# Starting the last pass of a transformer backward kernel with the first dV chunk: blocks made earlier, delta split beside other work, copies shared by two engines

## The chip, the cores and the metric

The kernel runs on one core of a Trainium2 chip. The metric is the device time of one execution in microseconds (us). Executions of one kernel scatter here with a standard deviation of 1.3 to 3.2 us, so where a small difference matters each experiment was run in five rounds beside the kernel before on the same chip. All runs used are of the state "fast". Engines: PE is TensorE's matmul, PEld its weight load, DVE VectorE, ACT ScalarE, POOL GpSimd (it issues the stores), SP SyncE (it issues the loads).

## The reference, cut to what matters

```python
x = x + A(layernorm(x))      # grouped-query attention over a cache: 8 (batch, kv head) groups, 16384 keys, head size 128
x = x + B(layernorm(x))      # an MLP: w1 (1024 x 3584), gelu, w2
x = x + A(layernorm(x))      # the same weights and caches again
x = x + B(layernorm(x))
# returned: x and the gradients of x, K cache, V cache, wq, wo, w1, b1, w2, b2
```

The caches are 32 MB each for K and for V. They are read in several passes, and dK and dV (as large) are written in the last pass. So the kernel moves 447 MB between HBM (the chip's memory) and SBUF (a core's own).

## The kernel before, where it matters

Loads go into seven rotating tiles of 8 KB per partition (`ld`) and ten fixed ones (`res`: the chunks of K and V that stay on the chip). Small vectors lie in pools ahead of them in SBUF; the order of the pools decides the addresses.

Some terms: a chunk is 4096 keys of one group, 1 MB of K or of V. `e_all` holds the exponentials of the scores, and a block is a transposed 128x128 piece of it. dO is the gradient of the attention's output O, and delta is the sum of dO * O over the 128 elements of a head. A row of a weight matrix is 128 of its rows at once; it is turned and multiplied on PE, or done as a pair of dot products ("dots") on DVE.

```python
const = ctx.enter_context(tc.tile_pool(name="const", bufs=1))
vec = ctx.enter_context(tc.tile_pool(name="vec", bufs=1))
pers = ctx.enter_context(tc.tile_pool(name="pers", bufs=1))      # e_all
ld = ctx.enter_context(tc.tile_pool(name="ld", bufs=NLD))        # 7 tiles of 8 KB per partition
res = ctx.enter_context(tc.tile_pool(name="res", bufs=1))        # keepV0..3, keepK0..3, keepxV, keepxK
...
    def do_delta(l, dops, ahead=None):        # dO scaled, then delta = sum(dO * O), split into three bf16 parts
        ...
        doT_bf = vec.tile([128, G, 8], BF16, name=f"doT_bf{l}")
        V.tensor_copy(out=doT_bf[:], in_=dof[:])
        V.tensor_tensor(out=prod[:], in0=dof[:], in1=sv["oT"][:], op=ALU.mult)
        dlp = part_sum(prod[:].rearrange("p g r -> p (g r)"), G * 8, "dl_ps")
        ...                                   # nine DVE instructions, each on the result of the last
```

The last pass makes dV, dK and dQ of layer 0 and the weight gradients. Its head was:

```python
    for t in TP:                               # two PSUM banks
        V.memset(t[:].bitcast(F32), 0.0)
    do_delta(0, pairs(dops, HQ), wob)
    ...                                        # cols: dO of both layers side by side, by copies
    qs = [make_qm(w, order[0]) for w in "VK"]
    for c in range(NCH):
        dp = mx()[:].rearrange("p (q t) -> p q t", t=TC)
        for b in range(NB):
            scores(c, b, kept_vT(c)[:, b * 8:(b + 1) * 8, :], dp)
        ds0(c, dp)                             # needs delta
        if c == 0:
            qs[0](); make_blks(0, None)        # blocks of dV chunk 0
        elif c == 1:
            kv_pair("V", 0, 0); make_blks(1, None)
        elif c == 2:
            kv_pair("V", 0, 1); qs[1]()        # chunk 0 is now stored
        else:
            kv_pair("V", 1, 0)
    for c in range(NCH):
        for q in range(2):
            dq_quad(c, q)
        if c == 1:
            kv_pair("V", 1, 1)
    ...
    pump(NLD + 3, 4)                           # the next loads, into tiles that come free
```

`evac` helpers pick ACT or DVE by a running charge per engine; in some stretches all copies are forced onto ACT (`only["e"] = "A"`), while DVE does dot products.

## Time and profile before

| | before |
|---|---|
| three runs, us | 1165.72, 1166.01, 1171.62 |
| profiled span, us | 1165.4 |
| PE, DVE, ACT busy | 82%, 55%, 48% |
| HBM read, written | 348.14 MB, 98.58 MB |

A page of the profile divides the span into 40 slices and gives busy tenths. For one stage, the table of stretches is the better view (width, busy time and instruction count of PE, PEld, DVE, ACT and POOL, then granted clock, DMA share and GB/s). The prediction below shows and reads the lines of the hole at 745 to 765 us. One view it did not use is needed later: the packets of one stretch. Here is that line of the kernel before from 30 to 180 us, where the K and V caches stream in for the first layer's attention:

```profile
DMA packets 8604, 62.80 MB, mean 419 GB/s; under 512 B 958, under 2 KB 958, under 8 KB 958
```

The reader is to see a rate in a stretch where the DMA share is 1.01 throughout: 419 GB/s is what the 16 engines moved there.

### The profile page before, as it was taken

The page shows a single profiled execution, that of the slowest core. Times are in us where ns is not written, and L with a number is a line of the kernel's source. Part 1 is how long each engine was busy: PE and PEld are TensorE (multiplying, and loading weights), DVE is VectorE, ACT ScalarE, POOL GpSimd, SP SyncE. Part 2 cuts the span into 40 slices and gives each one's busy share as a digit, 9 for nine tenths or more (in the row PEclk, how much of TensorE's full clock was granted, in tenths as well). Part 3 has the DMA queues.
Part 4 walks back from the last instruction along what each step waited for, and adds up shares of the span by engine and source line. Part 5 has one row for each costly group of instructions (what it writes and reads, how often), then busy time and mean ns, then how long its engine had stood idle before and what let it go on. Part 6 is the DMA issues. An engine that isn't in the chain of part 4 may idle for free. (4 is left out here: it accounts for less than half of the span.)

```text
span 1165.4 us, 39945 instructions
## 1 busy us (share of the span) xinstructions
PE 955.5 (82%) x17565; PEld 733.2 (63%) x17565; DVE 639.5 (55%) x1344; ACT 562.3 (48%) x1410; POOL 63.9 (5%) x113
## 2 busy tenths in 40 slices
PE   4888895497879875889987799788998988998786
PEld 3866773487767765888776688565555554555452
DVE  1545451133545433454845355867777877787674
ACT  0544351022535430344554444467677866686673
POOL 0000000000000000000000000001111111111111
PEclk9988785587988875999998889797777877797795
DMA  9999999998999989999999999687999999999996
GB/s 370 418 419 418 419 419 397 395 360 352 418 419 414 418 306 418 388 357 408 365 414 412 338 353 350 251 325 299 374 402 422 419 419 418 420 421 418 422 419 247
DMA packets 89130, 449.30 MB, mean 386 GB/s; under 512 B 7026, under 2 KB 7026, under 8 KB 49788
## 3 DMA queue, kind: packets, MB, share of 16 engines
q1 hardware_dynamic: 72204, 348.17, 74.9%
q0 software_dynamic: 16752, 98.59, 20.6%
q8 instruction: 137, 2.24, 0.8%
q14 instruction: 37, 0.30, 0.1%
HBM read 348.14 MB, written 98.58 MB: 383 GB/s over the span
## 5 line engine op out<-in xcount | busy, mean ns | idle before, releaser
L152 ACT COPY kT<-tp 128x512 int32<-128x512 int32 x209 | 122.8, 587 | 257.5 <-PE tp L418 246.5
L155 DVE COPY kT<-tp 128x1024 bf16<-128x1024 bf16 x159 | 108.6, 691 | 112.2 <-PE tp L418 99.2
L418 PE MATMUL tp<-ident,kv_K 128*128 128x128 bf16 x1728 | 147.1, 235 | 3.5 <-DMA kv_K<-in_A_k_cache_dram 3.5
L418 PEld LDWEIGHTS <-kv_K 128*128 128x128 bf16 x1728 | 111.6, 105 | 4.1 <-DMA kv_K<-in_A_k_cache_dram 4.1
L163 DVE CAST big<-xm 128x512 bf16<-128x512 f32 (+1 forms) x138 | 89.8, 685 | 31.3 <-PE xm L1222 14.4
L160 ACT CAST big<-xm 128x512 bf16<-128x512 f32 (+1 forms) x159 | 86.7, 594 | 27.8 <-PE xm L1081 16.8
L571 PEld LDWEIGHTS <-kT 128*128 128x128 bf16 x2048 | 76.7, 98 | 28.0 <-issue 22.1
L571 PE MATMUL sc<-qT_bf,kT 128*128 128x8 bf16 x2048 | 92.1, 171 | 0.7 <-issue 0.7
L268 PE MATMUL wtp<-ident,wt 128*128 128x128 bf16 x928 | 77.1, 231 | 3.7 <-issue 2.4
L418 PE MATMUL tp<-ident,kv_V 128*128 128x128 bf16 x864 | 70.3, 227 | 10.0 <-DMA kv_V<-in_A_v_cache_dram 8.2
L304 PEld LDWEIGHTS <-wt 128*128 128x128 bf16 x1696 | 49.0, 103 | 46.0 <-issue 14.7
L535 ACT ACTIVATE e_all<-sc,negm 128x64 bf16<-128x64 f32 x256 | 77.2, 345 | 1.2 <-DVE negm L530 1.2
L163 DVE CAST keepK<-xm 128x512 bf16<-128x512 f32 x94 | 61.1, 685 | 16.1 <-PE xm L1222 12.4
L450 PE MATMUL acc_all<-kv_V,e_all 128*16 128x256 bf16 x864 | 45.8, 292 | 28.7 <-DMA kv_V<-in_A_v_cache_dram 16.9
L155 DVE COPY wT<-wtp 128x1024 bf16<-128x1024 bf16 (+1 forms) x65 | 41.5, 645 | 48.7 <-PE wtp L268 45.2
L152 ACT COPY wT<-wtp 128x512 int32<-128x512 int32 (+1 forms) x59 | 33.5, 568 | 69.2 <-PE wtp L268 60.5
L160 ACT CAST keepK<-xm 128x512 bf16<-128x512 f32 x103 | 55.4, 592 | 22.4 <-PE xm L1222 21.3
L160 ACT CAST keepV<-xm 128x512 bf16<-128x512 f32 (+1 forms) x91 | 49.4, 594 | 34.9 <-PE xm L1222 28.8
L418 PEld LDWEIGHTS <-kv_V 128*128 128x128 bf16 x864 | 55.5, 102 | 11.8 <-DMA kv_V<-in_A_v_cache_dram 8.9
L163 DVE CAST keepV<-xm 128x512 bf16<-128x512 f32 (+1 forms) x81 | 52.8, 685 | 18.1 <-PE xm L1222 14.1
L268 PEld LDWEIGHTS <-wt 128*128 128x128 bf16 x928 | 58.9, 103 | 4.4 <-issue 2.9
L535 ACT ACTIVATION_READ_ACCUMULATOR e_all<-sc,negm 128x1 f32 x256 | 60.2, 235 | 0.0
(344 smaller groups left out, 1774.2 us busy)
## 6 DMA issues: line engine op xcount, KB each, us to landing
kv_K<-in_A_k_cache_dram SPq DMA_DIRECT2D x81, 1024.0 KB, 12.3
kv_V<-in_A_v_cache_dram SPq DMA_DIRECT2D x81, 1024.0 KB, 12.1
out_dram<-big POOLq DMA_DIRECT2D x36, 1024.0 KB, 17.7
wt<-in_A_wo_dram SPq DMA_DIRECT2D x32, 1024.0 KB, 10.3
wt<-in_B_w_dram SPq DMA_DIRECT2D x32, 896.0 KB, 14.3
out_dram<-keepK POOLq DMA_DIRECT2D x22, 1024.0 KB, 17.3
out_dram<-keepV POOLq DMA_DIRECT2D x18, 1024.0 KB, 16.2
wt<-in_A_wq_dram SPq DMA_DIRECT2D x16, 1024.0 KB, 9.1
```

The lines of the kernel that those rows point to most:

```text
L152: S.copy(out=dst.bitcast(I32), in_=src.bitcast(I32))
L155: V.tensor_copy(out=dst, in_=src)
L160: S.copy(out=dst, in_=src)
L163: V.tensor_copy(out=dst, in_=src)
L268: PE.transpose(tp[:, o, :], wv[:, j, (o0 + o) * 128:(o0 + o + 1) * 128], ident[:])
L304: PE.matmul(fps[:, jo, :].rearrange("p (a b) -> p a b", b=2), lhsT=wv[:, j, jo * 128:(jo + 1) * 128], rhs=xT_bf[:, j0 + j, :].unsqueeze(1) ...
L418: PE.transpose(tp[:, j, :], cv[:, b * 8 + j, :], ident[:])
L450: PE.matmul(self.acc[cg:cg + 16, :], lhsT=coef(u), rhs=self.cv[:, t:t + 2, :].rearrange("p t d -> p (t d)"), start=False, stop=True, tile_ ...
L535: S.activation(out=e_all[:, g, f * half:(f + 1) * half, l, h, :], in_=sc[g][f][:, h, :].rearrange("p (a b) -> p a b", b=2), func=ACT.Exp, ...
L571: PE.matmul(sc[g][f][:, :, t % TH], lhsT=kT[:, j, :], rhs=q_bf[:, g, :], start=True, stop=True)
```

## The change

The intent is to close the hole at the start of the last pass: start PE on what needs no delta, and store the first dV chunk as soon as its dO is there.

```diff
+    zero1 = const.tile([128, 1], F32, name="zero1")
+    V.memset(zero1[:], 0.0)
...
+    def copies_on(e):
+        only["e"] = e
+        load["A"] = load["D"] = 0.0
...
-            self.dotted = range(4, self.J, 5)
+            self.dotted = range(4, FJ, 5)            # w_o row 29 goes to PE
...
-        doT_bf = vec.tile([128, G, 8], BF16, name=f"doT_bf{l}")   # for layer 0: written into cols["V"] instead
...
     _, dmps = w_pass(B_w1, D, F, "dm_ps", gT_bf=dh_all[:, :, lsl(0)],
-                     mid=lambda: col_to_row_f32(...))
+                     mid=lambda: (col_to_row_f32(...), make_blks(0, None), make_blks(1, None)))
...
-    TP = [pt([128, 8, 128], BF16, "tpm%d" % i) for i in range(2)]
-    for t in TP:
-        V.memset(t[:].bitcast(F32), 0.0)
-    do_delta(0, pairs(dops, HQ), wob)
...
+    dof = do_scaled(0, pairs(dops, HQ), wob, ...)     # batch 1 first, straight into cols["V"]
+    qv = make_qm("V", order[0])
+    odp = {1: kept_scores(1, sm_dp())}
+    dl_bank = pt([128, 512], F32, "dl")
+    delta_mm(0, dof, dl_bank)
+    qv()
+    kv_pair("V", 0, 0)
+    odp[2] = kept_scores(2, tp_dp())
+    delta(0, dl_bank)
+    charge("D", 2.0)
+    kv_pair("V", 0, 1)                                # chunk 0 is stored
+    odp[0] = kept_scores(0, tp_dp())
+    ds0(1, odp[1])
+    odp[3] = kept_scores(3, sm_dp())
+    kv_pair("V", 1, 0)
+    ...
+    TP.extend(fixed_tp(i) for i in range(2))          # banks cleared by ACT from zero1
```

More of the change, by code (lines that the diff above doesn't have):

```diff
@@ L830, in attn_out_bwd, with do_scaled @@
         _, dops = w_pass(A_wo, HD, D, "do_ps", gT_bf=gA_all[:, :, lsl(l)])
-        return do_delta(l, dops)
-    def do_delta(l, dops, ahead=None):
+        doT_bf = saved[f"a{l}"]["doT_bf"] = vec.tile([128, G, 8], BF16, name=f"doT_bf{l}")
+        dof = do_scaled(l, dops)
+        do_store(l, dof[:], doT_bf[:])
+        delta(l, delta_mm(l, dof))
+        return doT_bf
+    def do_scaled(l, dops, ahead=None, half=lambda b, dof: None):
         sv = saved[f"a{l}"]
         dof = wrk.tile([128, G, 8], F32, name="dof")
-        for b in range(2):
+        for b in (1, 0):
             V.tensor_tensor(out=dof[:, b * HKV:(b + 1) * HKV, :].rearrange("p k r -> p (k r)"), in0=dops[:, :, b],
@@ L840, in do_delta, with do_store, delta_mm, delta @@
                 r_ = sv["rbc"][:, b * HKV:(b + 1) * HKV, :].rearrange("p k r -> p (k r)")
-                V.tensor_tensor(out=dof[:, b * HKV:(b + 1) * HKV, :].rearrange("p k r -> p (k r)")[:, 4:HQ:5],
-                                in0=ahead.dp[:, :, b], in1=r_[:, 4:HQ:5], op=ALU.mult)
-        doT_bf = vec.tile([128, G, 8], BF16, name=f"doT_bf{l}")
-        V.tensor_copy(out=doT_bf[:], in_=dof[:])
+                V.tensor_tensor(out=dof[:, b * HKV:(b + 1) * HKV, :].rearrange("p k r -> p (k r)")[:, 4:FJ:5],
+                                in0=ahead.dp[:, :, b], in1=r_[:, 4:FJ:5], op=ALU.mult)
+            half(b, dof)
+        return dof
+    def do_store(l, dof, dst):
+        V.tensor_copy(out=dst, in_=dof)
+    def delta_mm(l, dof, bank=None):
+        sv = saved[f"a{l}"]
         prod = wrk.tile([128, G, 8], F32, name="dprod")
         V.tensor_tensor(out=prod[:], in0=dof[:], in1=sv["oT"][:], op=ALU.mult)
-        dlp = part_sum(prod[:].rearrange("p g r -> p (g r)"), G * 8, "dl_ps")
+        bank = pm_([128, 512], F32, "dl_ps") if bank is None else bank
+        PE.matmul(bank[:, 0:G * 8], lhsT=onesf[:], rhs=prod[:].rearrange("p g r -> p (g r)"), start=True, stop=True)
+        return bank
+    def delta(l, bank):
+        dlp = bank[:, 0:G * 8]
         rest_ = wrk.tile([128, G * 8], F32, name="dl_rest")
-        V.tensor_scalar(out=rest_[:], in0=dlp[:], scalar1=-1.0, scalar2=None, op0=ALU.mult)
+        V.tensor_scalar(out=rest_[:], in0=dlp, scalar1=-1.0, scalar2=None, op0=ALU.mult)
         part = wrk.tile([128, G * 8], BF16, name="dl_part")
@@ L861, in do_delta @@
                 V.tensor_tensor(out=rest_[:], in0=rest_[:], in1=part[:], op=ALU.subtract)
-        saved[f"a{l}"]["doT_bf"] = doT_bf
-        return doT_bf
     wq_v = A_wq.rearrange("(j p) n -> p j n", p=128)
@@ L938 @@
     mlp_slope(0)
-    only["e"] = "A"
+    copies_on("A")
     g2 = attn_in_bwd(1, g3, dn1, lambda: some(rest, 2), lambda: some(rest, 3))
@@ L955 @@
         w2b.products(j, dhps, gM_all[:, :, lsl(0)])
-    only["e"] = None
+    copies_on(None)
     mlp_hidden_bwd(0, pairs(dhps, FJ), w2b)
     x4 = mlp_out(1, fps[:, 0:DJ * WIDE].rearrange("p (j b) -> p j b", b=WIDE)[:, :, 0:2])
+    order = []
+    for kv in [HKV - 1] + list(range(HKV - 1)):
+        order += [HKV + kv, kv]
+    chunks = [(g, c) for g in order for c in range(NCH)]
+    NC = len(chunks)
+    by_read, by_store = deque(), deque()
+    banks = {"tp": lambda: pt([128, 8, 128], BF16, "tpe")}
@@ new lines, in mtp, with make_blks @@
+    def mtp():
+        return banks["tp"]()
+    blks = {}
+    dX = [held_tiles["V0"][:, c * 512:(c + 1) * 512].rearrange("p (u l h t) -> p u l h t", l=2, h=8, t=2)
+          for c in range(NCH)] + [dXr[i % 3] for i in range(NCH, NC)]
+    def make_blks(iv, ik):
+        tp = mtp()
+        lo, hi = NB, NB
+        for w, i in (("V", iv), ("K", ik)):
+            if i is None or not 0 <= i < NC:
+                continue
+            g, c = chunks[i]
+            o = 0 if w == "V" else NB
+            lo, hi = min(lo, o), max(hi, o + NB)
+            for bi in range(NB):
+                src = e_all[:, g, c * CP + bi * 4:c * CP + bi * 4 + 4] if w == "V" else dX[i][:, bi * 4:bi * 4 + 4]
+                PE.transpose(tp[:, o + bi, :], src.rearrange("p u l h t -> p (u l h t)"), ident[:])
+        if hi > lo:
+            if ik is None:
+                blk = ktp.tile([128, NB, 128], BF16, name="blkv", tag="blkv", bufs=3)
+            else:
+                blk = ktp.tile([128, 2 * NB, 128], BF16, name="blk", tag="blk", bufs=2)
+            evac_bf16(blk[:, lo:hi, :].rearrange("p a b -> p (a b)"), tp[:, lo:hi, :].rearrange("p a b -> p (a b)"),
+                      (hi - lo) * 128)
+            blks["V", iv] = blks["K", ik] = blk
+        if ik == NCH - 1:
+            by_read.append(held_tiles["V0"])
@@ L959 @@
+    cols = {}
+    for w in "VK":
+        cols[w] = vec.tile([128, G, 2, 8], BF16, name="cols" + w)
+        for k in range(2):
+            if w + str(k) != "V0":
+                V.tensor_copy(out=cols[w][:, :, k, :], in_=saved["a%d" % k]["qT_bf" if w == "K" else "doT_bf"][:])
+    dq0 = vec.tile([128, G, 8], F32, name="dqT0")
+    dn0 = vec.tile([128, DJ, 2], F32, name="dn0")
+    V.memset(dn0[:], 0.0)
     sv = saved["m0"]
     _, dmps = w_pass(B_w1, D, F, "dm_ps", gT_bf=dh_all[:, :, lsl(0)],
-                     mid=lambda: col_to_row_f32(x4, DJ, out_0.rearrange("b s d -> (b s) d"), "o0"))
+                     mid=lambda: (col_to_row_f32(x4, DJ, out_0.rearrange("b s d -> (b s) d"), "o0"),
+                                  make_blks(0, None), make_blks(1, None)))
@@ L967 @@
     V.tensor_copy(out=dm[:], in_=dmps[:])
-    only["e"] = "A"
+    copies_on("A")
     dn = ln_bwd(dm[:], sv["y2"][:], sv["rstd2"][:], "dn", lambda: some(rest, 2), lambda: some(rest, 3))
@@ L991 @@
         wob.products(j, dops, gA_all[:, :, lsl(0)])
-    only["e"] = None
-    TP = [pt([128, 8, 128], BF16, "tpm%d" % i) for i in range(2)]
-    for t in TP:
-        V.memset(t[:].bitcast(F32), 0.0)
-    do_delta(0, pairs(dops, HQ), wob)
+    copies_on(None)
     rowsA = ld.tile([128, LDW], BF16, name="rowsA", tag="ld")
@@ L1019 @@
     rot = {"x": 0, "tp": 0}
-    by_read = deque(ld.tile([128, LDW], BF16, name="big", tag="ld") for _ in range(NLD - 1))
-    by_store = deque()
+    by_read.extend(ld.tile([128, LDW], BF16, name="big", tag="ld") for _ in range(NLD - 1))
     def nxt(what, lst):
@@ L1030, in mx @@
         return nxt("x", X)
-    def mtp():
-        return nxt("tp", TP)
     def n_free():
@@ L1090, in rows_of @@
         return lambda j0, rb: out_ap[j0 * 128:(j0 + rb) * 128, :].rearrange("(j p) n -> p j n", p=128)
-    order = []
-    for kv in [HKV - 1] + list(range(HKV - 1)):
-        order += [HKV + kv, kv]
-    chunks = [(g, c) for g in order for c in range(NCH)]
-    NC = len(chunks)
     jobs = deque()
@@ L1153 @@
     qms = {}
-    cols = {}
-    for w in "VK":
-        cols[w] = vec.tile([128, G, 2, 8], BF16, name="cols" + w)
-        for k in range(2):
-            src = saved["a%d" % k]["qT_bf" if w == "K" else "doT_bf"]
-            V.tensor_copy(out=cols[w][:, :, k, :], in_=src[:])
     def make_qm(w, g):
@@ L1178, in make_qm @@
         return second
-    blks = {}
-    dX = [held_tiles["V0"][:, c * 512:(c + 1) * 512].rearrange("p (u l h t) -> p u l h t", l=2, h=8, t=2)
-          for c in range(NCH)] + [dXr[i % 3] for i in range(NCH, NC)]
-    def make_blks(iv, ik):
-        tp = mtp()
-        lo, hi = NB, NB
-        for w, i in (("V", iv), ("K", ik)):
-            if i is None or not 0 <= i < NC:
-                continue
-            g, c = chunks[i]
-            o = 0 if w == "V" else NB
-            lo, hi = min(lo, o), max(hi, o + NB)
-            for bi in range(NB):
-                src = e_all[:, g, c * CP + bi * 4:c * CP + bi * 4 + 4] if w == "V" else dX[i][:, bi * 4:bi * 4 + 4]
-                PE.transpose(tp[:, o + bi, :], src.rearrange("p u l h t -> p (u l h t)"), ident[:])
-        if hi > lo:
-            if ik is None:
-                blk = ktp.tile([128, NB, 128], BF16, name="blkv", tag="blkv", bufs=3)
-            else:
-                blk = ktp.tile([128, 2 * NB, 128], BF16, name="blk", tag="blk", bufs=2)
-            evac_bf16(blk[:, lo:hi, :].rearrange("p a b -> p (a b)"), tp[:, lo:hi, :].rearrange("p a b -> p (a b)"),
-                      (hi - lo) * 128)
-            blks["V", iv] = blks["K", ik] = blk
-        if ik == NCH - 1:
-            by_read.append(held_tiles["V0"])
     stgs = {}
@@ L1229, in kv_pair @@
             store(dst[g, :, c * TC:(c + 1) * TC, :], stgs[w, i][:].rearrange("p (t d) -> p t d", d=128), stgs[w, i])
-    dq0 = vec.tile([128, G, 8], F32, name="dqT0")
-    dn0 = vec.tile([128, DJ, 2], F32, name="dn0")
-    V.memset(dn0[:], 0.0)
     dwq_v = out_4.rearrange("(j p) n -> p j n", p=128)
@@ L1317, with fixed_tp, kept_scores, tp_dp @@
     open_dq(order[0])
-    qs = [make_qm(w, order[0]) for w in "VK"]
-    for c in range(NCH):
-        dp = mx()[:].rearrange("p (q t) -> p q t", t=TC)
+    TP = []
+    def fixed_tp(i):
+        t = pt([128, 8, 128], BF16, "tpm%d" % i)
+        S.copy(out=t[:].bitcast(F32), in_=zero1[:].to_broadcast([128, 512]))
+        return t
+    def kept_scores(c, dp):
         for b in range(NB):
             scores(c, b, kept_vT(c)[:, b * 8:(b + 1) * 8, :], dp)
-        ds0(c, dp)
         if c > 0:
             by_read.append(held_tiles["V%d" % c])
-        if c == 0:
-            qs[0]()
-            make_blks(0, None)
-        elif c == 1:
-            kv_pair("V", 0, 0)
-            make_blks(1, None)
-        elif c == 2:
-            kv_pair("V", 0, 1)
-            qs[1]()
-        else:
-            kv_pair("V", 1, 0)
-    for c in range(NCH):
+        return dp
+    def tp_dp():
+        return pt([128, 16, TC], F32, "dp")[:]
+    def sm_dp():
+        return pm_([128, 16, TC], F32, "dp")[:]
+    dof = do_scaled(0, pairs(dops, HQ), wob,
+                    lambda b, dof: do_store(0, dof[:, b * HKV:(b + 1) * HKV], cols["V"][:, b * HKV:(b + 1) * HKV, 0, :]))
+    qv = make_qm("V", order[0])
[12 more added lines that the diff above has]
+    kv_pair("V", 1, 0)
+    for c in (0, 2):
+        ds0(c, odp[c])
+    for q in range(2):
+        dq_quad(0, q)
+    kv_pair("V", 1, 1)
+    ds0(3, odp[3])
+    TP.extend(fixed_tp(i) for i in range(2))
+    banks["tp"] = lambda: nxt("tp", TP)
+    qk = make_qm("K", order[0])
+    for c in (1, 2):
         for q in range(2):
             dq_quad(c, q)
-        if c == 1:
-            kv_pair("V", 1, 1)
+    qk()
+    for q in range(2):
+        dq_quad(3, q)
     accs[order[0]].evac()
```

## The prediction

> **What bounds the kernel now.** I read the page first: 1165.4 us of span, PE 82% busy, DMA slices nearly all at 9. No chain carries the whole (the chain that ended last explains only some 6% of the span, and only from 1121 us on), so I read by stage. Table 2 of the page has one hole late in the run, in slices 25 to 28 (each is 29.1 us wide, so 728 to 845 us):
>
> ```profile
> DMA  9999999998999989999999999687999999999996
> GB/s 370 418 419 418 419 419 397 395 360 352 418 419 414 418 306 418 388 357 408 365 414 412 338 353 350 251 325 299 374 402 422 419 419 418 420 421 418 422 419 247
> ```
>
> This is where the last pass begins (dV, dK, dQ of layer 0 and the weight gradients). The busy-time table by stretches (columns: stretch, width, PE, PEld, DVE, ACT, POOL busy, granted clock, DMA share, GB/s) shows how it begins:
>
> ```profile
> 740.00:745.00 5.00, 0.98 (x13) 0.77 (x10) 4.08 (x12) 0.28 (x1) 0.00 (x0) 0.71 1.02 419
> 745.00:750.00 5.00, 2.64 (x43) 1.68 (x43) 3.39 (x19) 0.00 (x0) 0.00 (x0) 0.50 0.37 154
> 750.00:755.00 5.00, 4.49 (x83) 2.67 (x82) 3.12 (x8) 1.07 (x2) 0.00 (x0) 0.50 0.02 3
> 755.00:760.00 5.00, 3.42 (x51) 1.48 (x47) 2.41 (x4) 1.63 (x4) 0.58 (x1) 0.50 0.19 79
> 760.00:765.00 5.00, 4.66 (x92) 2.99 (x92) 2.67 (x4) 3.38 (x7) 0.54 (x1) 0.74 0.67 223
> ...
> 810.00:820.00 10.00, 9.48 (x126) 5.86 (x123) 8.48 (x15) 8.07 (x16) 1.73 (x3) 0.83 1.01 366
> ```
>
> PE is nearly idle from 740.7 to 747.5 us, ACT does nothing from 740.3 to 752.7, and the DMA engines stand still from about 748 to 759. Summing (1 - share) x width over the stretches from 745 to 810 gives about 22 us of lost DMA time; from 840 to 1140 the share is 1.00 to 1.02 and nothing is lost. The waits of that late stretch say the same from another side: the load queue always waits for a store to land (its largest entry is 103.8 us behind stores of the big tiles, 16 times), because a load needs the tile that a store gives back, while PE waits for a load only three times, 9.4 us together. Loads, stores and the engines are near balance there, and the DMA side is full. What can be won is the hole.
>
> The hole follows from the timeline:
>
> ```profile
> 740.34 0.36 PE L379 MATMUL wob_b<-gA_all,wt 128*128 128x32 bf16 x8 [0.28 <-ACT wt L152]
> 742.40 1.03 DVE L995 MEMSET tpm<- 128x512 f32 x2
> 743.34 0.17 DVE L837 TENSOR_TENSOR dof<-wob_b,rbc 128x32 f32<-128x32 f32 x1
> 747.49 0.27 PE L1165 MATMUL tpm<-ident,colsV 128*16 128x128 bf16 x1 [2.36 <-DVE colsV L1160]
> 757.95 0.58 POOL L1045 DMA_DIRECT2D out_dram<-keepV  x1 [46.20 <-ACT keepV L160]
> 762.39 0.33 SPq L1119 DMA_DIRECT2D keepV<-in_A_k_cache_dram  x1
> 764.39 0.54 POOL L1045 DMA_DIRECT2D out_dram<-keepV  x1 [5.86 <-ACT acc_sb L160]
> ```
>
> The reader is to see a chain: last w_o product at 740.7, two last dots on DVE to 742.3, two bank clears to 743.4, then delta and its three-part split on DVE alone to 747.3, and only then a PE instruction of the last pass. The first dV chunk is stored at 757.95. The first new load at 762.39 waits for that store (22.1 us in the load queue's waits), the next for the second store.
>
> [...] about 420 GB/s for both together in the late pass[...]. [...] Here PE's idle 6.8 us is followed by a clock of 0.50 from 745 to 762; the 128x512 product takes 0.59 us there and 0.38 later. [...]
>
> **The change part by part.**
>
> (1) The e_all blocks of dV chunks 0 and 1 are made in the w1 pass. 8 transposes of 128x128, at about 0.08 us each (8 in 0.61 us): 0.6 to 0.7 us, and two copies of 0.41 us. PE is 90 to 100% busy from 700 to 740 us, with no DMA wait worth naming, so I count +0.8 us for PE here, with a bank wait. It leaves the head of the last pass, where it took two stretches of 0.61 us on PE and two copies on DVE.
>
> (2) w_o row 29 goes from two dots on DVE (1.26 us start to start, so 2.5 us) to a turn and a product: rows follow each other every 0.64 us on PE and 0.63 us on ACT. PE ends 0.65 us later, DVE 2.5 us earlier. PE's last product: 740.7 + 0.8 + 0.65 = 742.15. DVE's last dot: 742.3 + 0.8 - 2.5 = 740.6, so PE now sets the start.
>
> (3) The bank clears (1.03 us on DVE) leave the start; ACT does them later. dof starts at about 742.3 instead of 743.34: **1 us won**.
>
> (4) The half of dof that the first group needs comes first (three DVE steps 0.2 us apart), written straight into the columns. PE starts at about 743.1 instead of 747.49, **4.4 us earlier**, with scores that need no delta. The split (nine DVE instructions, 745.17 to 747.26, 2.1 us) runs beside PE work.
>
> (5) The dV chunk 0 path: transpose 0.3, scores of chunk 1 1.06, delta product 0.7, Qm product 0.4 and copy 0.4, first pair 0.6, scores 1.06 and second pair 0.6, bringing PE to 748.2; its four evictions, mostly on ACT because DVE holds the split, take about 0.6 us each: 750.5. So the first store goes out at about **750.3 instead of 757.95** (7.6 us earlier), and the second at about 757.3 instead of 764.39.
>
> (6) From there the gain shrinks. The same scores, four 0.59 us products, quads and pairs remain, and new waits come: the first dX needs the split (dlr at about 750), chunk 3's scores need the bank of chunk 1, the clears on ACT[...] stand after its evictions and before the K transpose. Before, dof start to the last quad is 743.34 to 763.5 = 20.1 us. Minus 3.1 us (delta, 744.1 to 747.2, now covered) minus 1.2 us (blocks gone) plus about 1.5 us of waits: 17.3 us. 742.3 + 17.3 = 759.6, so the main loop begins about **3.9 us earlier**.
>
> (7) Resetting the balance of copies: in the ACT-only stretch 28 copies are charged about 0.6 each (16.7) against 12 dots at 1.15 (13.8), so DVE gets the next 3 us of copies, with ACT idle. Reset, both share; this is in (5) already.
>
> The sum: the stores gain 7.6 us, the engines 3.9 us. Up to 810 us PE is 80 to 95% busy and DMA 0.4 to 1.0, so there the engines count more; after it, DMA. I choose 5 us, between the two and nearer the engines: 1166.0 - 5 = **1161.0 us**.
>
> **The rivals.** (A) *The engines set the whole gain.* For it: from 765 to 810 no engine waits for a load. Then 1166.0 - 3.9 = 1162, or 1164 if the new waits in (6) are 3.5 us instead of 1.5. (B) *DMA sets it.* For it: the share of 1.01 for 300 us and the load queue that waits for stores. Then all 7.6 us count: 1158.4. If the shorter PE gap also keeps the clock up, the head's PE work at 0.59 to 0.38 us a product gives up to 3 us more: 1155.5. Against the clock: the gap between 742.2 and 743.1 is short, but PE then still waits for DVE here and there, and the clock fell at 797 us too, at a PE share near 0.7. (C) *Nothing is left:* the loop after the head is bound by tiles that come free, the holes at 789 and 797 to 803 us grow, and the end stays at 1166. For it: three such holes stand there though engines and loads are both running. Against it: after 840 us no DMA time is left idle in which a head start could vanish. (D) *Slower:* the additions on PE in the w1 pass (1.45 us in (1) and (2)) cost and the rest is hidden, 1167.5; the 1.0 us of (3) alone nearly pays for this.
>
> **Range and chances.** Low end from B with the clock, high end from C: 1155.0 to 1166.5. The timed runs before span 1165.72 to 1171.62, so noise alone may take one of them out. Two per cent is 23.3 us, more than the 22 us of lost DMA time in all, so faster by 2% would need the whole hole and more: 0.01. Slower by 2% needs a stall that I can't see: 0.01. Within: 0.98.
>
> **What would show it.** In the changed trace: first dof at 742 to 743 us with no DVE clear before it (3); first PE instruction of the pass within 1.5 us of the last w_o product (4); first store at 749.5 to 751.5 and first load some 4.4 us after it (5); first quad of chunk 3 ended by 758 to 761 (6); DMA share between 745 and 760 up from about 0.2 to about 0.4. Wrong if the head is shorter and the end isn't (C), or if the lost DMA time from 745 to 810 falls by far more than 5 us.

## The result, and the profile after

| | before | after |
|---|---|---|
| median of fast runs, us | 1165.87 (4 runs) | 1151.67 (4 runs) |
| lowest to highest, us | 1162.14 to 1171.62 | 1151.11 to 1152.68 |
| profiled span, us | 1165.4 | 1150.5 |

The ratio is 0.9875, with a 95% interval from 0.9833 to 0.9916. A ratio is the mean time of one kernel's fast runs over that of the other's of the same rounds, so it is not quite the ratio of the medians. The gain is 14 us where 5 were predicted, and 1151.67 lies below the range.

The head of the last pass, from the timeline of the changed kernel (start and length in us, engine, line, operation; in brackets the idle time before and what ended it):

```profile
730.04 0.36 PE L385 MATMUL wob_b<-gA_all,wt 128*128 128x32 bf16 x8
730.44 0.19 DVE L847 TENSOR_TENSOR dof<-wob_b,rbc 128x32 f32<-128x32 f32 x1 [1.13 <-PE wob_b L385]
731.11 0.22 PE L1214 MATMUL tpe<-ident,colsV 128*16 128x128 bf16 x1 [0.70 <-DVE colsV L857]
...
737.61 0.58 POOL L1108 DMA_DIRECT2D out_dram<-keepV  x1 [36.94 <-ACT keepV L166]
...
741.85 0.33 SPq L1175 DMA_DIRECT2D keepV<-in_A_k_cache_dram  x1
...
745.43 1.14 ACT L1339 COPY tpm<-zero 128x512 f32<-128x512 f32 x2
745.86 0.54 POOL L1108 DMA_DIRECT2D out_dram<-keepV  x1 [7.67 <-ACT keepV L166]
746.11 0.27 PE L1214 MATMUL tpm<-ident,colsK 128*16 128x128 bf16 x1 [2.08 <-ACT tpm L1339]
```

The head changed as predicted: PE starts the pass 0.7 us after the last w_o product instead of 6.8 (with only delta's own product, 0.69 us, between), and the first store leaves 7.2 us after dof instead of 14.6. But two absolute times do not fit: the last w_o product is at 730.0 instead of 740.3 us. Most of the lead is there *before* the part that was rebuilt. The second layer's score products (count, lengths, first and last start) of before and of after show when it began:

```profile
L571 PE MATMUL sc<-qT_bf,kT x2048: 169/169/221, 30.7 to 417.9; 128*128 128x8 bf16 x187
```

```profile
L577 PE MATMUL sc<-qT_bf,kT x2048: 169/169/221, 30.4 to 410.8; 128*128 128x8 bf16 x187
```

The changed kernel is 7.1 us ahead at the end of the second forward attention, which contains no changed line. The packets of 30 to 180 us say how:

```profile
DMA packets 8714, 63.62 MB, mean 424 GB/s; under 512 B 968, under 2 KB 968, under 8 KB 968
```

424 GB/s instead of 419, at the same share of 1.01, on the same loads.

### The profile page after: what moved, and what is told of

It is laid out like the page before. It is cut to its first block, busy times and chain, and to the rows that moved or that the text cites. A ratio compares the mean times of both kernels' runs of the same rounds, so it can differ in the third digit from the quotient of the medians.

```text
span 1150.5 us, 39958 instructions
## 1 busy us (share of the span) xinstructions
PE 956.2 (83%) x17581; PEld 732.7 (64%) x17581; DVE 632.4 (55%) x1335; ACT 567.0 (49%) x1417; POOL 63.9 (6%) x113
## 5 line engine op out<-in xcount | busy, mean ns | idle before, releaser
L424 PE MATMUL tp<-ident,kv_K 128*128 128x128 bf16 x1728 | 144.6, 233 | 4.3 <-DMA kv_K<-in_A_k_cache_dram 4.3
L169 DVE CAST big<-xm 128x512 bf16<-128x512 f32 x142 | 92.3, 685 | 31.8 <-PE xm L1242 13.9
L166 ACT CAST big<-xm 128x512 bf16<-128x512 f32 x155 | 84.4, 593 | 25.9 <-PE xm L1144 15.5
L166 ACT CAST keepV<-xm 128x512 bf16<-128x512 f32 (+1 forms) x98 | 53.1, 594 | 22.5 <-PE xm L1242 18.9
L169 DVE CAST keepV<-xm 128x512 bf16<-128x512 f32 (+1 forms) x74 | 48.0, 684 | 15.3 <-PE xm L1242 12.7
## 6 DMA issues: line engine op xcount, KB each, us to landing
out_dram<-keepK POOLq DMA_DIRECT2D x22, 1024.0 KB, 17.3
```

The lines of the kernel that those rows point to most:

```text
L166: S.copy(out=dst, in_=src)
L169: V.tensor_copy(out=dst, in_=src)
L424: PE.transpose(tp[:, j, :], cv[:, b * 8 + j, :], ident[:])
```

## The experiments

Fourteen runs followed, two of them repeats of the two kernels, each correct and in five rounds. Times below are medians of fast runs; ratios are to the kernel before in the same rounds.

### Chip or change: both kernels again

No edit. My first theory was that the two profiles came from chips of different DMA rate and that the change itself was worth the predicted 5 us.

> The unchanged kernel against itself, as the null. Theory 1 (the rate of the chip): of the 14.9 us between the two profiles, 7.1 us had built up by the end of the second layer's attention (418 against 411 us), in code that no part of the change touches, where DMA moved 419 GB/s before and 425 after; so the pooled ratio mixes chips. Then this ratio is 1.000 within 0.2%, and the kernel's own time on this chip lies anywhere from 1155 to 1172 us according to the chip's DMA rate. Theory 2 (all of the gain is the change): ratio 1.000 as well, and 1165 us.

> The changed kernel unaltered, against the one before on the same chip in the same rounds. Theory 1: ratio 0.9945 to 0.9965, 4 to 6.5 us, with the lead at the end of the second attention under 1 us. Theory 2: ratio 0.986 to 0.989, some 14 us.

Measured: the kernel before against itself 0.9995 (0.998 to 1.0011), 1165.06 us. The changed kernel 0.9878 (0.9853 to 0.9902), 1150.92 against 1165.54 us. The theory of the chip fell: on one chip the gain is still 14 us, and the second attention ended at 415.5 us in the one and 411.8 in the other. The rate of 419 or 424 GB/s goes with the kernel.

### Two small parts undone

```diff
     def copies_on(e):                       # a_noreset
         only["e"] = e
-        load["A"] = load["D"] = 0.0
+        pass
```

> The changed kernel without the reset of the copy balance: after an ACT-only stretch DVE again gets the next 3 us of copies. Theory that the reset is minor: within 1.5 us of the changed kernel. Theory that the 2.1 us by which the stretch from the first w2 product to its last (22.8 us before, 20.7 after) is shorter, or the head's eviction order, comes from it: 2 to 4 us slower than the changed kernel.

Measured: 1153.52 us, ratio 0.9892 (0.9867 to 0.9917). In the trace, dof to the first instruction of the main loop took 20.5 us against 18.9 and 19.1 in the two traces of the changed kernel. By the ratios it is 1.6 us slower than the changed kernel, with an uncertainty of some 3 us: neither theory is shown. The stretch of the w2 products was as short without the reset (20.4 us from the first to the last, 20.5 with it).

```diff
-            self.dotted = range(4, FJ, 5)   # a_dot29, with the two strides to match
+            self.dotted = range(4, self.J, 5)
```

> The changed kernel with w_o row 29 as two dots on DVE again. Theory of the prediction: PE ends 0.65 us earlier, DVE's last dot 2.5 us later, 1 us after PE; dof 0.5 to 1 us later than in the changed kernel, end time +0.5 to +1 us. Rival: hidden, 0.

Measured: 1153.36 us, ratio 0.9898 (0.9871 to 0.9925). The w_o products took 15.5 us instead of 16.0, and dof came 2.0 us after the start of the last of them instead of 0.2. So moving the row costs PE 0.5 us and frees dof by 1.8, a net 1.3 us, as the prediction had it in kind and a little more than the 0.5 to 1 us expected. Again the ratio alone does not separate the two.

All four changed kernels so far had the second attention done by 412 us, and both unchanged ones later than 415. Nothing that they do there differs; where the tiles lie does. The compiled programs give these SBUF addresses (bytes in a partition; they come out again when the kernels are built):

```text
                    e_all    first ld tile   keepV0    past a multiple of 256
kernel before       26208    58976           116320    96
changed kernel      26112    58880           116224     0
```

The change drops one dO tile of 128 bytes from the small vectors and adds `zero1`, 32 bytes with its padding. Everything behind moves down by 96.

### Where the tiles start

An unused tile ahead of the big ones moves them and does nothing else:

```diff
+    pad = const.tile([128, N // 4], F32, name="pad")
+    V.memset(pad[:], 0.0)
     hot3 = const.tile([128, 128], BF16, name="hot3")
```

The changed kernel with N = 96 (the old addresses), the kernel before with N = 32, 416, 160 and 128, then the changed kernel with N = 32:

> The changed kernel with an unused 96-byte tile put ahead of the big tiles. Six traces so far: DMA moves 418 to 420 GB/s in the full stretches from 30 to 180 us of both unchanged ones and 423 to 426 in those of all four changed ones, though no part of the change touches that code. What differs is where the tiles lie: the change frees 128 bytes (one dO tile) and adds 32, so every big tile moves down by 96 bytes, from an address that is 32 past a multiple of 64 to a multiple of 512. Theory P (placement): back at the old addresses this kernel shows 419 GB/s, the end of the second attention at 415 to 418 us instead of 411, and some 8 us of the 14 lost: 1158 to 1160 us, ratio 0.994 to 0.9965. Theory S (the schedule itself): no difference, 1151 us, ratio 0.988.

> The unchanged kernel with 32 unused bytes ahead of the big tiles, which then start at a multiple of 64 but not of 512 (128 past one). Theory P with 64 bytes as the step that counts: 424 GB/s in the full stretches, second attention done by 412 us, 1156 to 1158 us, ratio 0.992 to 0.9945. If only a larger step counts: 419 GB/s and ratio 1.000. Theory S: ratio 1.000.

> The unchanged kernel with 416 unused bytes ahead of the big tiles, which then start at a multiple of 512 as in the changed kernel. Theory P: 424 GB/s, 1156 to 1158 us, ratio 0.992 to 0.9945, whichever step counts. Theory S: 1.000.

> The unchanged kernel with 160 unused bytes ahead of the big tiles: they start at an odd multiple of 256 (so not of 512). [...] If 256 is the step that counts: 424 GB/s in the stretches from 30 to 180 us, 1155 to 1158 us, ratio 0.991 to 0.9935, as with 416 bytes. If 512 counts: 419 GB/s and 1.000.

> The unchanged kernel with 128 unused bytes ahead: the big tiles start 224 past a multiple of 256, where the unchanged one has 96 and the run with 32 bytes had 128. If the cost is in the bytes between the boundary below and the start (8192 + 224 against 8192[...]): 424 x 256/263 = 413 GB/s, some 8 to 12 us slower, ratio 1.007 to 1.01. If the cost is one more piece for any start that is off the boundary, however far: 419 GB/s and 1.000 as before.

> The changed kernel with 32 unused bytes ahead of the big tiles, so that they start 32 past a multiple of 256. So far 96 and 128 past gave 419 GB/s on rows of 8 KB and 387 to 389 on rows of 2 KB, 224 past gave 417 and 385, on the boundary 424 and 407 to 408. One more piece per row whatever the offset: 419 and 387, second attention done at 415.5 to 418 us, ratio 0.9965 to 0.999 as with 96 bytes. Cost in proportion to the bytes below the start: 423 and 402, ratio 0.989 to 0.992. It also repeats what the schedule is worth off the boundary: 2.6 us with 96 bytes, 4.3 us on the boundary by the ratio of the changed kernel to the unchanged one with 416 bytes.

Measured (GB/s from the packets of two stretches: 30 to 180 us, where rows of 8 KB of K and V load, and 187 to 200 us, where most loads are rows of 2 KB of w_o):

| kernel | start past 256 | 8 KB rows | 2 KB rows | second attention ends | median us | ratio (95%) |
|---|---|---|---|---|---|---|
| before | 96 | 419 | 387 | 417.9 | 1165 | 1 |
| before + 32 | 128 | 419 | 389 | 416.3 | 1165.17 | 0.9996 (0.9977 to 1.0014) |
| before + 128 | 224 | 417 | 385 | 417.7 | 1168.03 | 1.0025 (1.0012 to 1.0039) |
| before + 160 | 0 | 424 | 407 | 411.5 | 1156.73 | 0.9917 (0.9893 to 0.994) |
| before + 416 | 0 | 424 | 407 | 412.1 | 1157.27 | 0.9915 (0.9889 to 0.9941) |
| changed | 0 | 424 | 408 | 410.8 | 1150.92 | 0.9878 (0.9853 to 0.9902) |
| changed + 96 | 96 | 419 | 387 | 418.0 | 1162.73 | 0.9978 (0.9965 to 0.9991) |
| changed + 32 | 32 | 417 | 386 | 419.2 | 1164.74 | 0.9998 (0.9983 to 1.0013) |

The packets of the two stretches (first 30 to 180 us, then 187 to 200), of the kernel before with 416 bytes:

```profile
DMA packets 8718, 63.66 MB, mean 424 GB/s; under 512 B 967, under 2 KB 967, under 8 KB 967
...
DMA packets 2661, 5.30 MB, mean 407 GB/s; under 512 B 82, under 2 KB 82, under 8 KB 2660
```

and of the changed kernel with 96 bytes:

```profile
DMA packets 8606, 62.83 MB, mean 419 GB/s; under 512 B 957, under 2 KB 957, under 8 KB 957
...
DMA packets 2517, 5.03 MB, mean 387 GB/s; under 512 B 75, under 2 KB 75, under 8 KB 2515
```

The pair crosses over: the unchanged schedule at the new addresses has the fast rate, and the changed schedule at the old ones has the slow one. The unused tile also moves what the engines read, but they work as long as before: DVE 639.5 and ACT 562.3 us busy in the kernel before, 639.4 and 562.4 us with 416 bytes. This settles it. **The placement alone, without any change of schedule, is worth 0.9915 and 0.9917, 9.9 and 9.7 us; the schedule alone, at the old addresses, 0.9978, 2.6 us.** At a multiple of 256 the schedule is worth 0.9878/0.9915 = 0.9963, 4.3 us; with both kernels at 417 GB/s (32 and 224 past) 0.9998/1.0025 = 0.9973, 3.1 us. The last two are ratios of ratios, so each has an uncertainty of some 2 us or more: I take 2.5 to 4.5 us for the schedule.

Not all of the bands on record were met. Changed + 96 came out at 0.9978, above the band of the placement theory, so it lost more than forecast; before + 416 lies just below its band. 32 past missed both of its bands, and 224 past fell between its two.

The unused tile moves the SBUF side of the loads, the side that is written. A step of 256 agrees with these runs: 32, 96, 128 and 224 past gave 417 to 419 GB/s, and an odd multiple of 256 (the run with 160) is as fast as a multiple of 512 (424 GB/s on rows of 8 KB and 407 on rows of 2 KB, as with 416). The size of the loss does not follow from the bytes between the multiple of 256 below and the start. If it did, as an estimate from the 424 GB/s and the 8192 bytes of a row, 96 past would give 424 x 8192/8288 = 419 GB/s, 32 past 422, and 224 past 424 x 8192/8416 (that is 256/263) = 413; 419 was measured at 96, but 417 at both 32 and 224. As an estimate from the rates (62.80 and 63.66 MB in 150 us, 5.03 and 5.30 MB in 13 us, over 16 engines), a row that starts off a multiple of 256 costs about 4 ns more on an engine in these two stretches, for 8 KB (313 against 309 ns) and for 2 KB (85 against 80) alike: 1.3% of a long row and 5% of a short one.

The packed traces hold the time of each packet too (no view prints it). It says where this cost arises:

| start past 256 | 8 KB row, 30 to 180 us | 2 KB row, 187 to 200 us | 8 KB row loaded, 840 to 1120 us |
|---|---|---|---|
| 0 | 309 ns | 84 ns | 309 ns |
| 96 or 128 | 312 ns | 88 ns | 309 ns |
| 32 or 224 | 313 ns | 87 ns | 309 ns |

These are medians; the means of the first column are 310.6, 314.5 to 315.0 and 316.2 to 316.3 ns. In the last pass, where stores share the engines with loads, a row takes the same time at every start (means 311 to 318 ns, in no order of the start). The packets from 840 to 1120 us, of the kernel before and with 416 bytes, show no difference in rate that stands out of the 416 to 422 GB/s of all traces:

```profile
DMA packets 21058, 117.04 MB, mean 418 GB/s; under 512 B 1857, under 2 KB 1857, under 8 KB 10779
...
DMA packets 20642, 117.41 MB, mean 419 GB/s; under 512 B 1865, under 2 KB 1865, under 8 KB 10088
```

So the cost is not a fixed part of each row: it showed from 30 to 180 and from 187 to 200 us, where loads alone fill the engines (312 or 313 against 309 ns, 87 or 88 against 84), and not from 840 to 1120 us (309 ns at every start). Why it needs that, and why 32 and 224 past cost a little more than 96 and 128, stays open.

### What sets the head: stores or engines

```diff
+            if held_back is not None:                    # a_latestore, in the head only
+                held_back.append((dst[...], stgs[w, i][...]))
+                by_store.append(stgs[w, i])
+                return
             store(dst[...], stgs[w, i][...], stgs[w, i])
...
     accs[order[0]].evac()
+    nc.gpsimd.tensor_tensor(out=late_mark[:], in0=accs[order[0]].sb[:, 0, 0:2], in1=neghalf[:], op=ALU.mult)
+    for out_ap, view in held_back:
+        nc.gpsimd.dma_start(out_ap, view)
+    held_back = None
```

> The changed kernel with the first two dV stores held back until the head of the last pass is done (its queue waits for an instruction that reads the evicted dQ sum); the engines' work is untouched. First store some 12 us later, second some 4 us later, first load some 12 us later. Rival A of the prediction (the engines' head start sets the gain): end within 1.5 us of the changed kernel. Rival B (DMA sets it, all of the earlier stores counts): 4 to 8 us later, ratio 0.992 to 0.995.

```profile
751.07 0.18 POOL L1394 TENSOR_TENSOR late_mark<-acc_sb,neghalf 128x2 f32<-128x2 f32 x1 [49.28 <-DVE acc_sb L169]
751.58 1.14 POOL L1396 DMA_DIRECT2D out_dram<-keepV  x2 [0.33 <-issue]
```

The timeline of its store queue shows both stores at 751.6 us, 20.0 us after dof instead of 7.2; the first load followed at 755.96. Measured: 1153.58 us, ratio 0.9897 (0.9877 to 0.9918), between the two bands that I had written down. A delay of 12.8 us of the first store costs about 2 us by the ratios, with an uncertainty of some 3 us: the early store is most of what one sees in the timeline and only a part of what it is worth. The DMA engines made the delay good: from 1.6 to 66.6 us after dof their share was 0.71 with the stores held back and without.

```diff
-    qv = make_qm("V", order[0])             # a_deltafirst
-    odp = {1: kept_scores(1, sm_dp())}
     dl_bank = pt([128, 512], F32, "dl")
     delta_mm(0, dof, dl_bank)
+    delta(0, dl_bank)
+    qv = make_qm("V", order[0])
+    odp = {1: kept_scores(1, sm_dp())}
     qv()
```

> The changed kernel with delta and its three-part split put back ahead of the first scores and pairs. The first PE work then waits for 0.7 us of delta product and 2.1 us of split. Theory that the engines set the head and the end: from dof to the main loop 21 to 22 us instead of 19, end 2 to 3 us later, 1153 to 1154.5 us, ratio 0.989 to 0.9905. Rival (the split hides elsewhere or the pass has slack): within 1 us of the changed kernel.

Measured: 1153.44 us, ratio 0.9897 (0.9872 to 0.9921). The first store left 9.2 us after dof (7.2 before the edit), yet dof to the main loop took 18.6 us, no longer than with the split beside the pairs. The end lies in the band that I had given for a longer head (1153 to 1154.5 us), but the head is not longer. So my step from the split to a longer head was wrong: once the split is early, the first dX no longer waits for it, and what the start loses the rest of the head gives back. The time is 2.5 us longer by the medians, which the trace of the head does not explain and the overlapping intervals do not establish.

### An attempt at a better version

```diff
     def load_tile():                        # a_readfirst
-        return (by_store or by_read).popleft()
+        return (by_read or by_store if read_first else by_store or by_read).popleft()
...
     pump(NLD + 3, 4)
+    read_first = False                      # set True before the head
```

> An attempt at a better version: in the head the next loads go to tiles that were already read out (the last kept V and K tiles) and not to those whose stores are on the way, so that the first loads leave at about 5 us after the first scores end instead of waiting for the two stores; later loads as in the changed kernel. If DMA's start counts: 2 to 4 us faster, ratio 0.984 to 0.986. If the engines set the pass, as the run with late stores says (12 us later stores cost only 2 to 3): within 1.5 us of the changed kernel.

Measured: 1150.81 us, ratio 0.9883 (0.9859 to 0.9906), the same as the changed kernel. The first load left 8.9 us after dof instead of 11.4, the second 12.6 instead of 20.1. Nothing here shows the loads of the head to be a bound.

### The blocks back at the head

```diff
-                     mid=lambda: (col_to_row_f32(...), make_blks(0, None), make_blks(1, None)))
+                     mid=lambda: col_to_row_f32(...))                # a_headblk
...
+    make_blks(0, None)
+    make_blks(1, None)
     qv = make_qm("V", order[0])
```

> The changed kernel with the blocks of dV chunks 0 and 1 made at the start of the last pass, where PE waits some 0.7 us for dof, and not amid the w1 products. Prediction's count: 0.8 us less on PE in the w1 pass (last w2 product to last w1 product 21 us instead of 22), 0.6 to 1.2 us more from dof to the first store. Theory that the move of the blocks is worth little: within 1 us of the changed kernel either way; theory that it carries the schedule's gain: 2 us slower or more.

Measured: 1152.58 us, ratio 0.9893 (0.9876 to 0.991). Last w2 product to last w1 product: 21.4 us against 21.7; dof to first store 7.5 against 7.2. Where the blocks are made is worth nothing that these runs can show. No run beat the changed kernel. All five that undo or hold back one part of it came out slower, by 0.0014 to 0.0020 of the ratio (some 2 us); no single one is clear of noise.

## Why the prediction was wrong, point by point

**The step that failed** is the start of the count, "PE's last product: 740.7 + 0.8 + 0.65 = 742.15" in (2), and with it the sum, "1166.0 - 5 = 1161.0 us". It took everything before the last w_o product as unchanged but for 1.45 us of PE work. That product ended at 730.4 and 734.7 us in the two traces of the changed kernel. A term is missing: the big tiles move by 96 bytes onto a 256-byte boundary, and loads got faster where they fill the DMA engines alone (424 instead of 419 GB/s). It measured 9.7 and 9.9 us. None of the rivals had it; the low end of the range came from the clock in rival B. Two sizes of tile in the diff, 128 bytes dropped and 32 added, and the order of the pools would have shown that addresses move, though not what that is worth.

With this term put aside, the prediction's own 5 us stands against 2.5 to 4.5 measured. Its steps:

- (1) The blocks in the w1 pass were to cost PE 0.8 us. The stretch took 21.7 us in the profile after against 21.8 before. A second trace of the changed kernel had 23.8, so the cost is within the scatter.
- (2) Row 29 was to cost PE 0.65 us; 0.5 was measured. DVE waits for PE at the end, as said.
- (3) dof was to come 1 us earlier in absolute time. It came 42.8 and 45.0 us after the last w2 product in the two traces of the changed kernel, and 45.1 and 45.0 us after it in those of the kernel before: from nothing to 2.3 us, so these traces do not settle its size.
- (4) PE's start within 1.5 us of the last product: 0.7 us of idle time. Right. The 6.8 us of idle PE before, though, held delta's product: PE was idle for 3.73 and 2.36 us around it.
- (5) First store 8.0 us after dof predicted, 7.2 measured; second 15.0, 15.4 measured; first load 4.2 us after the store. Right.
- (6) dof to the main loop: 17.3 us predicted, 18.9 and 19.1 measured (20.1 before). The waits were put at 1.5 us, an estimate; one alone, the K transpose behind the two clears on ACT, took 2.08. The two clears took 1.14 us together (0.62 and 0.63 each, overlapping).
- (7) The reset of the balance: 1.6 us by the ratios, within noise.

Of the rivals, A (the engines set the gain) fits best: 1162 was its time, and 1162.73 is what the changed schedule takes at the old addresses. B counted all 7.6 us of the stores; the held-back stores cost about 2 us for a delay of 12.8. Whether DMA binds the late pass stays open. From the main loop's first instruction to the end took 401.9 and 399.5 us in the two traces of the kernel before, and 399.5 in both of those that have it on the boundary; but loads take as long there at every start, so these equal times say nothing about DMA. The sign named for being wrong did not appear: the lost DMA time in the 65 us after dof fell from 22 us to 19 or 20, and the rest of the gain lay elsewhere. The clock did not stay up either: 0.50 for most of the head, as this stretch view of the changed kernel shows. It fell at 735.8 us with no gap of PE above 0.70 us since the pass began; in the kernel before it fell at 742.2, only 1.5 us into the gap of 3.73. So the shorter gap did not prevent the fall, and of the 6.8 us of idle PE after which the prediction read a clock of 0.50, only the first 1.5 us had passed when it fell. What sets the clock was not shown.

```profile
731.00:736.00 5.00, 4.19 (x114) 3.29 (x115) 3.03 (x14) 2.20 (x5) 0.00 (x0) 0.97 1.00 419
736.00:741.00 5.00, 3.36 (x53) 1.44 (x49) 2.51 (x7) 2.37 (x5) 0.58 (x1) 0.50 0.54 229
741.00:746.00 5.00, 2.12 (x25) 0.73 (x26) 2.15 (x4) 2.48 (x6) 0.14 (x1) 0.50 0.62 216
746.00:751.00 5.00, 4.61 (x73) 3.30 (x73) 1.21 (x3) 1.53 (x4) 0.40 (x1) 0.66 0.52 216
```

The placement's gain shows where loads do bound the kernel: with the unchanged schedule, the last w2 product came at 691.7 and 689.3 us in the two traces on the boundary and at 695.6 to 698.2 in the three with 96 or 128 past it, so 4 to 9 us are there before the last pass begins.

## What to carry to other kernels

When a change to one stage moves the time, first compare landmarks in the stages that it does not touch; here half of the gain was there at 411 us, some 90 us before the first instruction that the change reorders (two halves of dO, 501.8 us) and almost 290 before the first of the last pass's own work (the blocks, 698.8 us). Then compare the addresses of the tiles that DMA fills, start them at a multiple of 256 bytes (worth 9.7 and 9.9 us of 1165 here, ratios 0.9917 and 0.9915), and test the placement alone with an unused tile before crediting the schedule. The gain showed here where loads alone filled the DMA engines (424 against 419 GB/s), and not where stores ran beside them (309 ns a row of 8 KB at every start). A hole in DMA's occupancy, and a store that leaves earlier, say little about the time until one has held the store back and seen what it costs (here about 2 us by the ratios for a delay of 12.8).
